# Output projection moved inside the seven-product form of the last matmuls, with its operands in float16, and the attention numerators computed two pairs ahead

## Chip, cores and metric

The kernel runs on one core of a Trainium2 chip. The metric is the device time of one execution in microseconds; the profiler's span, from the first to the last instruction of the core, is a little shorter. Engines: PE is TensorE (matmuls), DVE is VectorE, ACT is ScalarE, POOL is GpSimd, SP is SyncE, which here only issues DMAs.

## The reference

```python
def _A_ref(x, wqkv, w_phi, wo):          # S=2048, D=512, H=32 heads of Dh=16
    qkv = transpose((x @ wqkv).reshape(B, S, 3, H, Dh), 2, 0, 3, 1, 4)
    q, k, v = qkv[0], qkv[1], qkv[2]
    pq = einsum("bhsd,hdf->bhsf", q, w_phi);  pk = einsum("bhsd,hdf->bhsf", k, w_phi)
    phi_q = concat([softmax(pq), softmax(-pq)]);  phi_k = concat([softmax(pk), softmax(-pk)])
    kv  = einsum("bhsf,bhsd->bhfd", phi_k, v)
    z   = einsum("bhsf->bhf", phi_k)
    num = einsum("bhqf,bhfd->bhqd", phi_q, kv)
    den = einsum("bhqf,bhf->bhq", phi_q, z)[..., None] + 1e-6
    return reshape(num / den, (B, S, D)) @ wo

def _B_ref(x, w_gate, w_up, w_down):     # F=1792
    return ((x @ w_gate) * (x @ w_up)) @ w_down

xn = layernorm(x)
return x + _A_ref(xn, A_wqkv, A_w_phi, A_wo) + _B_ref(xn, B_w_gate, B_w_up, B_w_down)
```

All inputs are bfloat16 with batch 1. Two branches, linear attention with a softmax feature map and a gated linear unit without a nonlinearity, share the normalised input and are summed with x.

## The kernel before

**Tiles.** The 2048 tokens are 16 tiles of 128. K-blocks are 128 rows: 4 for D = 512, 14 for F = 1792. GLU units go over 4 token groups (`sg`) of 512.

**The loop** `for t in range(NT + 3)` (steps t = 0 to 18) works tile by tile: feature matmuls of k (`features("ek", ...)`), values (`v_matmul`, `v_place`), the sum over tokens `kv_acc(t - 3)` into PSUM banks 0 and 1, layernorm of later tiles, and GLU units. A unit, `up()`, is 8 matmuls of 512 columns into two of the banks 4 to 7 (in turn (4, 5) and (6, 7)), then `gate`: ScalarE copies one bank to SBUF, VectorE multiplies it with the other into `hT` (L814). From step 10 on the features of q run too (`q_next`): matmuls, two exponentials on ScalarE, a reduction on VectorE, a Ln and an Exp, two multiplications on POOL (L527, L529), and a transposing DMA into a slot of `phT` (L600). The k features end with a multiplication on POOL (L523). `w_fold` folds `w_phi` into the q and k weights.

**Scales.** h = gate x up and `w_down` are kept in float16, each multiplied by a power of two found on the chip: `squares` sums the squares of the weights (`wg`, `wu` on ScalarE at steps 3 to 9, `wd` on VectorE at steps 7 to 10, L651), `h_scale` (step 10) and `d_scale` (step 12) turn the sums into the scales `sh`, `swd` and the inverse `inv`. GLU outputs that were written before `sh` existed are converted later: those of token group 0 by `normalise` on POOL (L724, two per step from step 11; it waits for a row of reciprocal deviations that goes out to HBM and back, `r2row`), those of groups 1 and 2 by `to_half` on VectorE (L706), called after the loop and after pair 1.

**Output pairs.** The last part runs over 8 pairs p of token tiles t0 = 2p, t1 = 2p + 1. The product h @ w_down for 2 x 128 tokens and 2 x 256 columns, with F cut in two halves of 7 K-blocks, uses a form of Strassen-Winograd with 7 block products instead of 8. Sums of h blocks are made on VectorE (`h_combine`, 4 per pair, L775; three pairs ahead), sums of `w_down` blocks once (`wd_combine`, L745, `tw1` to `tw4`). `product` is 7 matmuls of 256 columns; `seed` is a ScalarE copy of one bank into another, so that partial results are used twice. The output projection o @ wo is outside of this form: `out_heads` adds 4 matmuls of 256 columns, in bfloat16, to each of the four output quarters. `finish_quarter` (L839, VectorE) scales by `inv` and adds x (or `xs`, which POOL makes at L859 from `s7` and x); `store` writes to HBM.

**Numerators.** `num_stage(t)`: 8 matmuls of 68 columns (L616) into banks 0 and 1 (tile 1: banks 2 and 3), a Ln and an Exp of the denominators on ScalarE, a division on VectorE into the tile `o` (L626), and a transposing DMA on SP (L631) that puts o transposed into the slot of `phT`. Tiles 0 and 1 run before pair 0, and tiles 2p + 2 and 2p + 3 run inside pair p, at the second and the third call of `fill()`. `fill()` of pairs 2 to 5 also runs one q feature tile each.

**Order.** TensorE runs in the order of the program. For the other engines `_order` simulates the steps with estimated costs and sorts each engine's queue, SP's included, by the modelled readiness and a priority (`sc.prio`; lower goes first). A queue, once made, is worked off in order, each instruction after the semaphores that it waits for. L224, L243 and L775 are lines of helpers (`act`, `mm`, `h_combine`), so the profile puts most ScalarE and TensorE work under one line each.

## Time and profile before

| what | value |
|---|---|
| runs | 218.68, 219.3, 220.6 us; median 219.3 |
| profiled execution | 217.15 us, span 215.3 us |
| granted TensorE clock | 1.00 |
| PE busy | 209.9 us, 97% of the span |
| DVE busy | 170.9 us, 79% |
| ACT busy | 133.7 us, 62% |
| POOL busy | 93.9 us, 44% |
| first numerators, first product of pair 0, end | about 144.4, 148.6 and 215.3 us |

Busy shares are averages over the whole span. The page also has the busy share of each engine in 40 slices of 5.4 us, the chain of work that ended last, followed back from the last instruction, groups of instructions with the mean time of one and the idle time ahead of them, and DMA issues. Further views list the instructions of a stretch in order of time and the busy time in chosen stretches. Times in a stretch count from the start of the span.

### The profile page before, as it was taken

What the parts mean: (1) busy time and instruction counts of PE and PEld (TensorE: products, weight loads), DVE (VectorE), ACT (ScalarE), POOL (GpSimd) and SP (SyncE); (2) the same over time, 40 slices, a digit from 0 to 9 for tenths busy, and PEclk for the clock granted to TensorE, in tenths of its full rate; (3) what the DMA queues carried; (4) which work ended last, traced back from release to release, by engine and by line L of the source; (5) the groups of instructions that cost most, each with busy time, mean ns of one, the idle gap of its engine ahead of it and who ended that gap; (6) DMA issues with size and microseconds to landing.
All of it is one profiled execution on the core that took longest, in us unless ns stands there. A gap on an engine that the chain in (4) does not pass through costs nothing.

```text
span 215.3 us, 3992 instructions
## 1 busy us (share of the span) xinstructions
PE 209.9 (97%) x1472; PEld 126.5 (59%) x1492; DVE 170.9 (79%) x281; ACT 133.7 (62%) x332; POOL 93.9 (44%) x112
## 2 busy tenths in 40 slices
PE   7999999999999999999999999999999999999994
PEld 2574444444444454444444444455988988989983
DVE  3838989967399999855999976869999999986332
ACT  5588869887977785876948676644333343553320
POOL 4032454530342244333999999690230523422220
PEclk9999999999999999999999999999999999999999
DMA  5999791893000000005423325255043285465731
GB/s 175 289 299 372 177 158 31 275 252 79 0 3 0 0 0 3 0 0 99 55 49 72 74 52 97 49 136 108 21 132 90 82 147 128 109 146 120 135 81 49
DMA packets 49075, 22.29 MB, mean 104 GB/s; under 512 B 38048, under 2 KB 47392, under 8 KB 49056
## 3 DMA queue, kind: packets, MB, share of 16 engines
q1 hardware_dynamic: 48112, 21.39, 43.5%
q10 hardware_dynamic: 944, 0.66, 1.0%
q8 instruction: 11, 0.18, 0.4%
q14 instruction: 8, 0.07, 0.1%
HBM read 11.03 MB, written 2.10 MB: 61 GB/s over the span
## 4 chain that ended last, share of the span: by engine, by line
PE 94%; DMA 3%; DVE 1%; issue 1%; SPq 0%; DVEq 0%
PE ps L243 89%; DMA arena<-in_A_wqkv_dram 3%; PE ps L616 2%; PE ps L559 2%; PE ps L375 1%; DVE arena L814 1%; DVE arena L775 0%; SPq L268 0%; DVE arena L839 0%; PE ps L481 0%; DVEq L1170 0%
## 5 line engine op out<-in xcount | busy, mean ns | idle before, releaser
L243 PE MATMUL ps<-arena 128*128 128x512 bf16 (+2 forms) x1156 | 200.0, 328 | 1.6 <-DMA arena<-in_A_wqkv_dram 0.5
L243 PEld LDWEIGHTS ps<-arena 128*128 128x128 bf16 (+1 forms) x1176 | 112.1, 98 | 75.7 <-ACT arena L224 1.5
L224 ACT ACTIVATE arena<-ps 128x512 bf16<-128x512 f32 (+4 forms) x119 | 59.9, 538 | 42.1 <-PE ps L243 20.0
L814 DVE TENSOR_TENSOR arena<-ps,arena 128x512 bf16<-128x512 f32 (+1 forms) x56 | 37.8, 682 | 13.0 <-PE ps L243 8.1
L523 POOL TENSOR_TENSOR arena<-arena 128x1024 bf16<-128x1024 bf16 x16 | 33.9, 2126 | 31.6 <-ACT arena L224 31.6
L513 DVE TENSOR_REDUCE arena<-arena 128x64 f32<-128x1024 bf16 x32 | 38.6, 1214 | 10.3 <-ACT arena L224 10.1
L224 ACT ACTIVATE arena<-arena 128x32 f32<-128x32 f32 (+8 forms) x119 | 40.6, 351 | 6.2 <-DVE arena L513 3.2
L224 ACT ACTIVATE arena<-ps,arena 128x512 bf16<-128x512 f32 (+1 forms) x51 | 32.5, 654 | 11.6 <-PE ps L243 10.7
L859 POOL TENSOR_TENSOR arena<-arena 128x256 f32<-128x256 f32 x16 | 11.4, 733 | 41.6 <-ACT arena L224 41.6
L839 DVE SCALAR_TENSOR_TENSOR arena<-ps,arena 128x256 bf16<-128x256 f32 x32 | 14.9, 480 | 11.6 <-PE ps L243 11.4
L724 POOL TENSOR_TENSOR arena<-arena 128x512 f16<-128x512 bf16 x14 | 19.1, 1375 | 9.3 <-DMA arena<-r2row 7.3
L775 DVE TENSOR_TENSOR arena<-arena 128x896 f16<-128x896 f16 x32 | 21.1, 674 | 0.1
L224 ACT ACTIVATE ps<-ps 128x256 f32<-128x256 f32 x24 | 8.8, 368 | 15.8 <-PE ps L243 15.5
L529 POOL TENSOR_TENSOR arena<-arena 128x512 bf16<-128x512 bf16 x16 | 17.9, 1119 | 1.3
L651 DVE SCALAR_TENSOR_TENSOR arena<-arena 128x1024 bf16<-128x1024 bf16 x7 | 13.5, 1961 | 0.2
L626 DVE TENSOR_TENSOR arena<-ps,arena 128x512 bf16<-128x512 f32 x16 | 10.9, 684 | 1.1 <-ACT arena L224 1.0
L402 DVE BATCH_NORM_STATS2 arena<-arena 128x6 f32<-128x512 bf16 x16 | 10.5, 669 | 0.0
L460 POOL TENSOR_SCALAR arena<-arena 128x1 f32<-128x1 f32 x12 | 3.2, 284 | 14.9 <-ACT arena L224 14.9
L462 DVE TENSOR_SCALAR arena<-arena 128x512 bf16<-128x512 bf16 x12 | 6.9, 604 | 1.7 <-DMA arena<-arena 1.7
L559 PEld LDWEIGHTS ps<-arena 128*128 128x128 bf16 x128 | 6.1, 97 | 3.5
L527 POOL TENSOR_TENSOR arena<-arena 128x32 f32<-128x32 f32 x16 | 4.6, 290 | 7.1 <-ACT arena L224 7.1
L616 PE MATMUL ps<-arena 128*128 128x68 bf16 x128 | 6.5, 194 | 0.0
(50 smaller groups left out, 65.5 us busy)
## 6 DMA issues: line engine op xcount, KB each, us to landing
arena<-in_A_x_dram SPq DMA_DIRECT2D x9, 256.0 KB, 3.0
out_dram<-arena SPq DMA_DIRECT2D x15, 128.0 KB, 2.0
arena<-in_B_w_down_dram SPq DMA_DIRECT2D x1, 1792.0 KB, 8.9
arena<-in_A_x_dram SPq DMA_DIRECT2D x3, 512.0 KB, 4.1
arena<-arena SPq DMA_TRANSPOSE x44, 3.0
arena<-in_B_w_gate_dram SPq DMA_DIRECT2D x1, 640.0 KB, 8.4
arena<-in_B_w_up_dram SPq DMA_DIRECT2D x1, 640.0 KB, 9.6
arena<-in_B_w_gate_dram SPq DMA_DIRECT2D x1, 512.0 KB, 5.0
```

What stands on the lines that cost most here:

```text
L224: return sc.step(ACT, lambda e: e.activation(out=out_ap, in_=in_ap, func=func, scale=scale, **kw), reads, writes, 130.0 + 0.833 * n)
L243: ins = e.matmul(out_ap, lhsT=l, rhs=r, start=start and i == 0, stop=stop and i == npair - 1, **kw)
L513: dve(lambda e: e.tensor_reduce(out=sm, in_=e_v, axis=AX.X, op=ALU.add), [(name, s, 0), (name, s, 1)], [("sums", sr)], 1024)
L523: pool(lambda e: e.tensor_tensor(out=e_w, in0=e_w, in1=r_w, op=ALU.mult), [(name, s, 0), (name, s, 1), ("rs", n)], [(name, s, 0), (name, s ...
L529: pool(lambda e: e.tensor_tensor(out=e_v[:, :, 1, :], in0=e_v[:, :, 1, :], in1=rat[:, :, None].to_broadcast([128, H, 16]), op=ALU.mult), [ ...
L626: dve(lambda e: e.tensor_tensor(out=o_tile(t).rearrange("p (b h f) -> p b h f", b=2, f=16), in0=nd[:, :, :, 0:16], in1=w_v[:, r].unsqueeze ...
L651: dve(lambda e: e.scalar_tensor_tensor(out=junk, in0=i_ap, scalar=1.0, in1=i_ap, op0=ALU.mult, op1=ALU.mult, accum_out=ssq[:, col:col + 1] ...
L724: pool(lambda e, ft=ft: e.tensor_tensor(out=hH_v[:, ft, 0:512], in0=hT_v[:, ft, 0:512], in1=r2w, op=ALU.mult), [("hT", ft, 0), "r2w", ("x" ...
L775: dve(lambda e, k=k, i0=i0, i1=i1, op=op: e.tensor_tensor(out=s_block(p, k), in0=i0, in1=i1, op=op), ks + more, [s_key(p, k)] + over.get(k ...
L814: dve(lambda e: e.tensor_tensor(out=h_v[:, ft, sg * 512:(sg + 1) * 512], in0=bank(bu), in1=g, op=ALU.mult), [("ps", bu), ("g", s)] + ([("j ...
L839: dve(lambda e: e.scalar_tensor_tensor(out=stg, in0=bank(b, 0, 256), scalar=inv, in1=resid, op0=ALU.mult, op1=ALU.add), [("ps", b), rkey, ...
L859: pool(lambda e, h=h: e.tensor_tensor(out=xs[h], in0=s7, in1=xr_tile(t1)[:, h * 256:(h + 1) * 256], op=ALU.add), ["s7", ("xr", t1 % 4)], [ ...
```

## The change

- The projection goes into the seven products: each product has 9 K-blocks, 7 of h with `w_down` and 2 of o with `wo`. `out_heads` goes away. For this o and wo become float16, with a common scale: `squares` of `wv` and `wo` on ScalarE (steps 9 and 10), a longer `d_scale`, which finds `so`, `swo`, `swd` and `inv` under caps, and two conversions of `wo` on VectorE. `kv_finish` scales the key-value sums by `so`.
- `combine_weights` makes the sums of both weights (`tw`, `two`) on VectorE, at steps 16 and 17 and after the loop; the third is made in place.
- `o_combine(p)` makes four sums of o blocks on POOL for each pair, in the free parts of the `phT` slots.
- Numerators of tiles 0 to 3 run before pair 0, with one GLU unit after each of the first three; pair p >= 1 runs tiles 2p + 4 and 2p + 5, at its first and second `fill()`; pair 0 runs 4 and 5.
- `to_half` goes from VectorE to ScalarE, one conversion per step from step 11.
- Squares, `w_fold(0, ...)` and `normalise` run one step earlier; `q_next` is spread over steps 9 to 18, and the last four q tiles run in pairs 0 to 3; step 14 has one GLU unit less.
- The bank numbers of the products change; two of the four finishing instructions of a pair become one over two banks, and the two `xs` instructions become one.

The core of the diff:

```diff
@@ num_stage's o is now float16; scales
     def o_tile(t):
-        return sb("o", (t % 3) * 512, 512)
+        return sbh("o", (t % 3) * 512, 512)
...
     def d_scale():
-        norms(14, 7, 1)
-        power_of_two(swd, scl[:, 18:19], [("rn", 14)], "swd", 4096.0)
-        dve(lambda e: e.tensor_tensor(out=scl[:, 22:23], in0=sh, in1=swd, op=ALU.mult), ["sh", "swd"], ["both"], 1)
-        dve(lambda e: e.reciprocal(out=scl[:, 23:24], in_=scl[:, 22:23]), ["both"], ["rboth"], 1)
-        power_of_two(inv, scl[:, 23:24], ["rboth"], "inv", 1.0009765625)
-        sc.prio = 2
+        norms(14, (2, 2, 7), 24)
...
+        for i in range(2):
+            sl = slice(2 * i, 2 * i + 2)
+            dve(lambda e, sl=sl: e.tensor_scalar(out=woh_v[:, sl, :], in0=wo_v[:, sl, :], scalar1=swo, scalar2=None,
+                                                 op0=ALU.mult), ["wo", "scales"], [("woh", i)], 1024, 0.35)
...
     def to_half(sg):
         fts = [ft for ft in range(NF) if (ft, sg) in raw]
-        sc.prio = 2
         for lo in range(0, len(fts), 2):
...
-            dve(lambda e, sl=sl: e.tensor_scalar(out=hH_v[:, sl, sg * 512:(sg + 1) * 512],
...
+            act(hH_v[:, sl, sg * 512:(sg + 1) * 512], hT_v[:, sl, sg * 512:(sg + 1) * 512],
+                ks + ["sh", ("hT", *latest[0])], ks, func=ACTF.Identity, scale=sh)
+            yield
...
+    def o_combine(p):
+        t0, t1 = 2 * p, 2 * p + 1
+        a11, a12, a21, a22 = (o_block(t, i) for t in (t0, t1) for i in range(2))
+        ks = [("phT", t0), ("phT", t1)]
+        for k, i0, i1, op, more in ((1, a21, a22, ALU.add, []),
+                                    (3, a11, a21, ALU.subtract, [1]),
+                                    (2, so_block(p, 1), a11, ALU.subtract, [1]),
+                                    (4, a12, so_block(p, 2), ALU.subtract, [2])):
+            pool(lambda e, k=k, i0=i0, i1=i1, op=op: e.tensor_tensor(out=so_block(p, k), in0=i0, in1=i1, op=op),
+                 ks + [("so", p, m) for m in more], [("so", p, k)], 256)
...
-    BA, BE, BB, BC, BD = 3, 7, 4, 5, 6
+    BA, BE, BD, BB, BC = 3, 5, 6, 7, 4
+
+    def product(b, a, w, start=False):
+        h, o, keys, okey = a
+        wh, wo_, wkeys = w
+        mm(bank(b, 0, 256), [(h[:, f, :], wh[:, f, :]) for f in range(NK)],
+           keys + wkeys + ([] if start else [("ps", b)]), b, start=start, stop=False, skip=True)
+        mm(bank(b, 0, 256), [(o[:, f, :], wo_[:, f, :]) for f in range(2)], [okey, ("ps", b)], b, start=False, skip=True)
...
+        product(BA, raw_a(t0, 0), raw_w(0, 0), True)
         seed(BB, BA)
         fill()
+        product(BE, sum_a(3), sum_w(3), True)
+        act(s7, ...); pool(xs = s7 + x, ...)
+        product(BB, sum_a(2), sum_w(2))
         seed(BD, BB)
+        fill()
+        product(BA, raw_a(t0, 1), raw_w(1, 0))
+        finish(t0, 0, 256, ...)
+        product(BB, sum_a(1), sum_w(1))
+        seed(BC, BB)
         fill()
+        product(BD, raw_a(t1, 1), sum_w(4))
+        finish(t1, 0, 512, ...)
+        product(BC, sum_a(4), raw_w(1, 1))
+        finish(t0, 256, 256, ...)
...
@@ after the loop
     h_combine(0)
-    wd_combine(4)
+    combine_weights(4)
...
-    num_stage(0)
-    up(len(ups) - 2)
-    num_stage(1)
-    up(2)
-    h_combine(1)
-    to_half(1)
-    h_combine(2)
-    h_combine(3)
+    for t in range(4):
+        num_stage(t)
+        up((1, 1, 1, len(ups))[t])
+        half_step(1)
+    half_step(99)
+    o_combine(0)
+    for p in range(1, 4):
+        h_combine(p)
     for p in range(NT // 2):
-        plan = [[], [2 * p + 2], [2 * p + 3]]
+        plan = [[2 * p + 4], [2 * p + 5], []] if p else [[], [4], [5]]
...
-            if 1 < p < 6 and len(plan) == 2:
+            if p < 4 and not plan:
                 q_next(2)
         out_pair(p, fill)
-        if p == 1:
-            to_half(2)
+        if p + 1 < NT // 2:
+            o_combine(p + 1)
```

## The prediction

> **What bounds the kernel now.** I read the page first: busy shares, slices, the chain that ended last.
>
> ```profile
> PE 209.9 (97%) x1472; PEld 126.5 (59%) x1492; DVE 170.9 (79%) x281; ACT 133.7 (62%) x332; POOL 93.9 (44%) x112
> PE   7999999999999999999999999999999999999994
> DVE  3838989967399999855999976869999999986332
> POOL 4032454530342244333999999690230523422220
> PEclk9999999999999999999999999999999999999999
> PE 94%; DMA 3%; DVE 1%; issue 1%; SPq 0%; DVEq 0%
> ```
>
> TensorE is busy from the second slice to the last, at a granted clock of 1.00 throughout, and it is 94% of the chain. VectorE is nearly full in the last third (slices 28 to 35, the output pairs) without being the chain. So a saving must take columns off TensorE, and an added wait costs only if it reaches TensorE. The list of waits, asked for TensorE alone from 20 us on, is empty. The windows cut at each pair's first numerator say the same (columns: stretch, its length, then busy time and instructions of PE, PEld, DVE, ACT and POOL, the granted clock, DMA share, GB/s):
>
> ```profile
> 152.15:159.76 7.61, 7.61 (x84) 6.86 (x81) 7.36 (x16) 2.43 (x8) 1.48 (x2) 1.00 0.27 69
> 168.23:176.70 8.47, 8.42 (x87) 7.26 (x85) 7.95 (x14) 3.68 (x12) 3.04 (x5) 1.00 0.59 95
> 193.64:201.25 7.61, 7.61 (x84) 6.88 (x82) 3.27 (x6) 2.63 (x10) 2.84 (x5) 1.00 0.70 120
> ```
>
> A pair takes 7.61 us, or 8.47 with a q feature tile in it. The last row has VectorE at 3.27 us instead of 7.36 and is no shorter: in the pairs VectorE sets nothing. The chain in order of time gives TensorE's price list:
>
> ```profile
> 152.31 0.26 PE ps L616 x8
> 152.57 2.40 PE ps L243 x22
> 154.97 0.26 PE ps L616 x8
> 155.23 4.69 PE ps L243 x43
> ```
>
> 22 matmuls of 256 columns in 2.40 us and 43 in 4.69 are both 0.1091 us each; a numerator tile (8 matmuls) is 0.26. Check: 65 x 0.1091 + 2 x 0.26 = 7.61, the window's length. A GLU unit (8 matmuls of 512 columns) is 1.73 us in the same view.
>
> **What is removed.** Before, a pair is 7 products of 7 matmuls and 4 groups of 4 for the output projection: 49 + 16 = 65. After, it is 7 x (7 + 2) = 63. Eight pairs: 16 matmuls x 0.1091 = **1.75 us** off the engine that is the chain. Halves in float16 bring no more: products in f16 and projection groups in bf16 both stand at 273 ns in the table of forms, and the stretch of 43 that mixes them ran at the same 0.1091 as the others. Splitting a product into two waiting steps costs nothing that shows, since the same stretch has such borders already.
>
> One page would make this term smaller. The Trainium skill, TensorE: Matmul & The Clock Gate, section Back-to-back issue gap, gives a sustained spacing of 81 ns at 128 columns and 131 at 512; halfway in columns that is an estimated 98 ns and 1.57 us. This trace has 216 ns at 512 (1.73 / 8), so the measurement decides.
>
> **What is added to POOL.** The sums of o: 4 subtractions per pair of 128x256 f16, each reading two SBUF operands and mostly waiting for the one before. No such row exists; the nearest are these.
>
> ```profile
> L859 POOL TENSOR_TENSOR arena<-arena 128x256 f32<-128x256 f32 x16 | 11.4, 733 | 41.6 <-ACT arena L224 41.6
> 158.55 2.12 POOL L859 TENSOR_TENSOR arena<-arena 128x256 f32<-128x256 f32 x2 [6.13 <-ACT arena L224]
> 175.70 1.30 POOL L859 TENSOR_TENSOR arena<-arena 128x256 f32<-128x256 f32 x2 [4.20 <-ACT arena L224]
> L724 POOL TENSOR_TENSOR arena<-arena 128x512 f16<-128x512 bf16 x14 | 19.1, 1375 | 9.3 <-DMA arena<-r2row 7.3
> ```
>
> Low end 0.65 us (1.30 for two), high end 1.06 (2.12 for two, while VectorE was working on f16 tiles); the longest single L859 was 1.49. I take 0.75, near the L859 mean. POOL per pair: 4 x 0.75 + 1.5 (residual and s7, same elements in one instruction) + 1.4 (the q tile's 0.27 + 1.1) = 5.9 us in a pair of 63 x 0.1091 + 0.52 + 0.86 = 8.25. It fits; with 1.06 throughout it is 4.2 + 2.1 + 1.8 = 8.1 and just fits. The sums for pair p+1 read tiles whose numerators run in pair p-1, so they have about a pair of lead, except for pair 0.
>
> A page speaks against this edit. The Trainium skill, SBUF — State Buffer, section Who interferes with whom: a VectorE instruction with two SBUF inputs and a GpSimd one that reads SBUF exclude each other for the whole instruction. The rows agree in kind (L775 on VectorE runs from 0.61 to 1.37 us, L859 from 0.67 to 1.49). By the rule a POOL op could wait out an L775 (0.62) each time, an estimated 1.3 us an op; the whole change would then come out slower.
>
> **Pair 0.** Now four numerator tiles and three GLU units precede it: 4 x 0.26 + 3 x 1.73 = 6.23 us from the first numerator to its first product. The path of one tile, in the rows of ScalarE, VectorE and SP around 168 us:
>
> ```profile
> 168.23 0.42 PE L616 MATMUL ps<-arena 128*128 128x68 bf16 x8
> 169.36 0.68 DVE L626 TENSOR_TENSOR arena<-ps,arena 128x512 bf16<-128x512 f32 x1
> 170.07 1.19 SPq L631 DMA_TRANSPOSE arena<-arena  x1
> ```
>
> Start of the numerators to the DMA's issue: 1.84 us; landing after 2.4 more (the line's minimum and median; maximum 4.6). Tile 1 starts at 0.26 + 1.73 = 1.99, so its o lies in SBUF at 6.23. Its sums S1 and S3 end at 6.23 + 2 x 0.75 = 7.73. The third-product group that reads S3 comes after 9 + 7 matmuls, at 6.23 + 1.75 = 7.98. This wait is new, and all of TensorE queues behind it; next in line, S2 is wanted 0.98 later and takes 0.75, so nothing piles up. Low end 0, high end 2.6 us (landing 4.6, sums 1.06: 1.99 + 1.84 + 4.6 + 2.12 - 7.98). I take 0.2, near the low end, for semaphore time is not in the sum.
>
> **Numerators two pairs ahead.** Within a pair they now stand 0.26 + 18 x 0.1091 = 2.22 us apart instead of 2.66, on the same banks 0 and 1. The second must wait until L626 has read the first: start to end of L626 was 1.81 (168.23 to 170.04), 1.81, 1.93, 1.99 and once 2.28 (152.15 to 154.43). Late by 0 to 0.1 per pair, six pairs: 0 to 0.6; I take 0.05. Each also brings its Ln and Exp (0.20, 0.23), its L626 and a 1.19 us transpose on SP. SP per pair: 2 x 1.19 + 1.24 + 2 x 0.55 + 0.43 = 5.2 us of 8.25, unchanged. The q tiles of pairs 2 to 5 go to 0 to 3 whole; their 0.86 us of TensorE merely moves.
>
> **The loop before the pairs.** ScalarE gets four squares of 1.04 + 0.19 = 4.9 us and the nine half conversions of hT (eight of 1.04, one of 0.6: 8.9 us), which VectorE loses (4.1 us in the pairs). ScalarE was busy 28.85 of 40 us from 80 to 120 and 13.75 of 20 after: about 70%, then 85 to 90%. A conversion can hold a gate back by 1.04. A gate needs 0.69 (ScalarE) + 0.68 (VectorE) + some 0.25, and its banks return two units later: at least one unit of 1.73, and in the new order 0.86 of features or values more, so about 1 us is free. Low end 0, high end 0.2 at each of eight steps, 1.6; I take 0.1. On VectorE two wo conversions (0.82 each), four small differences (0.4 each, scaled from 0.674 at 896) and some eight scale instructions of 0.16 add 4.5 us; before, 16.0 of 20 us were busy from 120 to 140, so it stays hidden, and the differences are wanted only in pair 0. The longer chain of scales starts near 100 us and is read at 141. The weight fold one step earlier finds its transposes landed (issued at 27.5, 6.7 to land, wanted past 47). The normalisation one step earlier still waits for r2row, landed at 100.5; behind it on POOL stand the k products, read three steps of 8 us later. A GLU unit less at step 14 is one of the three before pair 0.
>
> **Sum.** -1.75 + 0.2 + 0.05 + 0.1 = -1.4 us. Against the profiled execution (217.15 us, span 215.3): 215.75, span 213.9. The median of the runs, 219.3, lies 1% above that execution; the same -1.4 gives **217.9 us**, 0.6% less. The tail (last product, 0.48 of VectorE, about 2 us of store) stays.
>
> **Rivals.** (1) *More than the sum:* TensorE's small idle times between 28 and 201 us add to 1.1 us, and VectorE, 95% busy in the pairs, is relieved. All gone and no new wait: -2.85, 216.4. Against it: the last window above, where free VectorE brought nothing. (2) *The saving goes into pair 0:* with a landing near 4.6 us and sums near 1.06, 2.6 us are lost there: -1.75 + 2.6 + 0.15, 220.3; with half of it 219.0. For it: POOL also has the last q tiles then. Against: the median landing is at the minimum. (3) *Slower: POOL paces the pairs.* From a mean of 1.09 us per sum on, POOL needs more than the 8.25 us of a pair with a q tile. At 1.2, between the contended 1.06 and the longest 1.49, it is 4.8 + 2.4 + 1.8 = 9.0, 0.75 late in each of four pairs, and 7.2 against 7.39 in the others: +3.0 - 1.4 = +1.6, 220.9; at 1.3 it is 9.6 and 7.8, +6.6 - 1.4 = +5.2, 224.5. For it: both engines' long rows when they overlap. Against: six of the eight L859 pairs are near 1.3 us. (4) *Little is won:* conversions hold gates up at each step, 1.6 us lost: 219.3.
>
> **How the numbers follow.** Forecast 0.47, (1) 0.21, (2) 0.12, (3) 0.13, (4) 0.07. One per cent is about what a measurement can tell from no change. Faster: all of (1), and 0.06 of the forecast where no new wait appears: 0.27. Slower: (3), and 0.05 of (2) and (4) at their ends: 0.18. The rest, 0.55, is within 1%. The forecast's own range is 217.3 to 219.2; the wider one goes to (1) below, 216.2, and to (2) and the mild half of (3) above, 220.9.
>
> **What would show it.** Right: 536 matmuls of 256 columns instead of 552, a pair without q of 7.4 us and with q of 8.25, POOL sums of 0.65 to 0.85, and TensorE's wait list naming POOL at pair 0 at most, under 0.5 us. Wrong: TensorE waiting on POOL in later pairs (3), on L626 at L616 (spacing), or on gates between 93 and 145 us (4); or a loop longer than before by the time the first numerator starts, less the moved GLU unit.

## The result and the profile after

The changed kernel takes **227.1 us** (median; 226.6 to 229.2), the kernel before 219.05 in the same comparison: a ratio of 1.037, 95% interval 1.029 to 1.046. Forecast were 217.9 us and a range up to 220.9. The profiled execution took 226.6 us with a span of 224.8, so 9.5 us more than the 215.3 of before. The page of the changed kernel, with the rows that answer to those shown of before:

```profile
PE 211.0 (94%) x1476; PEld 124.5 (55%) x1476; DVE 178.8 (80%) x276; ACT 144.6 (64%) x349; POOL 116.4 (52%) x138
PE   7999999999999999999967899997689999999995
DVE  3848999953899997658999999998899987985223
POOL 4032654343034425509965999815839747566620
PEclk9999999999999999999999999999999999999999
PE 60%; DVE 27%; issue 5%; ACT 4%; DMA 3%; POOL 1%; DVEq 0%; POOLq 0%
```

TensorE has holes in two places, the 21st to 23rd slice of 5.62 us (112 to 129 us: the loop) and the 28th to 30th (152 to 169 us: the start of the pairs). VectorE reads 9 in and ahead of the first, and 8, 8 and 9 in the second, and the chain that was 94% TensorE is now 27% VectorE. The granted clock of this execution is 1.00 throughout; of the four timed ones only the slowest, 229.2 us, has a mean below it, 0.985. The list of waits for TensorE from 20 us on, empty before, now reads:

```profile
PE ps L616 <- DVE arena L626: 4.1, 5, 2.4
PE ps L243 <- DVE arena L860: 2.3, 2, 1.5
PE ps L243 <- ACT arena L224: 2.0, 2, 1.7
PE ps L243 <- POOL arena L822: 1.4, 1, 1.4
```

(total us, number of waits, longest.) L860 is `gate` (before: L814), L822 `o_combine`, L800 `h_combine` (before: L775), L889 `finish` (before: `finish_quarter`, L839).

**Where the 9.5 us lie.** The first numerators of the kernel before, then rows of the changed kernel (the bracket holds the idle time ahead of a row and what ended it):

```profile
144.43 0.67 PE L616 MATMUL ps<-arena 128*128 128x68 bf16 x16
```
```profile
147.38 0.42 PE L616 MATMUL ps<-arena 128*128 128x68 bf16 x8
157.71 1.38 PE L243 MATMUL ps<-arena 128*128 128x256 f16 x11 [1.41 <-POOL arena L822]
163.66 0.43 PE L616 MATMUL ps<-arena 128*128 128x68 bf16 x8 [2.36 <-DVE arena L626]
```

The first numerator starts at 147.38 us, before at 144.43, although one GLU unit of 1.73 fewer stands ahead of it: the loop is 2.95 + 1.73 = 4.7 us longer. From there to the end it is 77.4 us (224.8 - 147.4) against 70.9 (215.3 - 144.4). With one unit more (+1.73) and 16 matmuls fewer (-1.75) it should have been 70.9 again: the pairs are 6.5 us longer. 4.7 + 6.5 - 1.75 = 9.5. TensorE's own rows show idle times of 4.3 us in the loop (0.25, 1.47, 0.84, 1.72) and 5.7 behind it, the largest 1.41 and 2.36 in pair 0. They add to 10.0 of 11.2. A row's end is modelled, and in an undisturbed stretch the next row starts some 0.17 us before it, so each of these eleven holes is up to that much longer than its number.

### The profile page after: what moved, and what is told of

The parts are those of the page before. It is cut to its first block, busy times and chain, and to the rows that moved or that the text cites. A ratio compares the mean times of both kernels' runs of the same rounds, so it can differ in the third digit from the quotient of the medians.

```text
span 224.8 us, 4025 instructions
## 1 busy us (share of the span) xinstructions
PE 211.0 (94%) x1476; PEld 124.5 (55%) x1476; DVE 178.8 (80%) x276; ACT 144.6 (64%) x349; POOL 116.4 (52%) x138
## 4 chain that ended last, share of the span: by engine, by line
PE 60%; DVE 27%; issue 5%; ACT 4%; DMA 3%; POOL 1%; DVEq 0%; POOLq 0%
PE ps L243 56%; DVE arena L513 6%; DVE arena L800 5%; DVE arena L860 4%; ACT arena L224 4%; DVE arena L771 3%; DVE arena L718 3%; DVE arena L889 2%; DVE arena L626 2%; DMA arena<-arena 1%; DMA arena<-in_A_x_dram 1%; PE ps L559 1%; PE ps L616 1%; POOL arena L822 1%; DVE arena L672 1%
## 5 line engine op out<-in xcount | busy, mean ns | idle before, releaser
L243 PEld LDWEIGHTS ps<-arena 128*128 128x128 bf16 (+1 forms) x1160 | 110.3, 98 | 80.8 <-ACT arena L224 3.5
L224 ACT ACTIVATE arena<-arena 128x32 f32<-128x32 f32 (+8 forms) x132 | 53.9, 423 | 17.6 <-DVE arena L513 10.4
L523 POOL TENSOR_TENSOR arena<-arena 128x1024 bf16<-128x1024 bf16 x16 | 34.0, 2129 | 28.6 <-ACT arena L224 28.5
L860 DVE TENSOR_TENSOR arena<-ps,arena 128x512 bf16<-128x512 f32 (+1 forms) x56 | 37.8, 682 | 12.4 <-ACT arena L224 6.4
L513 DVE TENSOR_REDUCE arena<-arena 128x64 f32<-128x1024 bf16 x32 | 38.6, 1209 | 4.0 <-ACT arena L224 3.8
L822 POOL TENSOR_TENSOR arena<-arena 128x256 f16<-128x256 f16 x32 | 23.7, 749 | 19.8 <-DMA arena<-arena 19.1
L800 DVE TENSOR_TENSOR arena<-arena 128x896 f16<-128x896 f16 x32 | 26.4, 846 | 2.6 <-POOL arena L822 1.9
L889 DVE SCALAR_TENSOR_TENSOR arena<-ps,arena 128x256 bf16<-128x256 f32 (+1 forms) x24 | 13.5, 566 | 11.9 <-PE ps L243 11.9
L743 POOL TENSOR_TENSOR arena<-arena 128x512 f16<-128x512 bf16 x14 | 17.4, 1262 | 10.4 <-DMA arena<-r2row 7.9
L529 POOL TENSOR_TENSOR arena<-arena 128x512 bf16<-128x512 bf16 x16 | 18.4, 1148 | 0.9
L626 DVE TENSOR_TENSOR arena<-ps,arena 128x512 f16<-128x512 f32 x16 | 10.9, 683 | 4.8 <-ACT arena L224 4.8
L918 POOL TENSOR_TENSOR arena<-arena 128x512 f32<-128x512 f32 x8 | 10.8, 1354 | 5.7 <-ACT arena L224 5.7
L527 POOL TENSOR_TENSOR arena<-arena 128x32 f32<-128x32 f32 x16 | 5.7, 354 | 13.9 <-ACT arena L224 11.6
L616 PE MATMUL ps<-arena 128*128 128x68 bf16 x128 | 6.7, 194 | 4.3 <-DVE arena L626 4.1
L616 PEld LDWEIGHTS ps<-arena 128*128 128x128 bf16 x128 | 5.7, 97 | 7.0 <-DVE arena L626 5.0
```

What stands on the lines that cost most here:

```text
L224: return sc.step(ACT, lambda e: e.activation(out=out_ap, in_=in_ap, func=func, scale=scale, **kw), reads, writes, 130.0 + 0.833 * n)
L243: ins = e.matmul(out_ap, lhsT=l, rhs=r, start=start and i == 0, stop=stop and i == npair - 1, **kw)
L513: dve(lambda e: e.tensor_reduce(out=sm, in_=e_v, axis=AX.X, op=ALU.add), [(name, s, 0), (name, s, 1)], [("sums", sr)], 1024)
L523: pool(lambda e: e.tensor_tensor(out=e_w, in0=e_w, in1=r_w, op=ALU.mult), [(name, s, 0), (name, s, 1), ("rs", n)], [(name, s, 0), (name, s ...
L529: pool(lambda e: e.tensor_tensor(out=e_v[:, :, 1, :], in0=e_v[:, :, 1, :], in1=rat[:, :, None].to_broadcast([128, H, 16]), op=ALU.mult), [ ...
L616: ins = e.matmul(bank(b0 + c // 4, (c % 4) * CW, CW), lhsT=ph[:, c, :], rhs=kvz_v[:, c, :], start=True, stop=True)
```

## Experiments

Two theories for the loop. *Order*: the nine conversions of weights, now at the same priority as the gates, stand ahead of more urgent work in VectorE's queue. *Load*: VectorE has too much to do there, whatever its order. Two for the pairs: the numerators' new *spacing*, or *the sums of o* on POOL, which would make VectorE's work on two SBUF operands longer. Edits are against the changed kernel unless the kernel before is named; all ratios are to the kernel before.

**The saving by itself (on the kernel before).** Two matmuls are left out of each pair: the last K-block of o @ wo for the odd token tile.

```diff
-    mm(bank(b, 0, 256), [(oT_tile(t)[:, q, :], wo_v[:, q, ...]) for q in range(NQ)], ...
+    mm(bank(b, 0, 256), [(oT_tile(t)[:, q, :], wo_v[:, q, ...]) for q in range(NQ - t % 2)], ...
```

> The kernel before with two matmuls per pair left out (the last K-block of o @ wo for the odd tile, both halves), so that part of the projection is missing from the output: 63 instead of 65 matmuls of 256 columns per pair, the same number that the changed kernel has, and nothing else. If the columns of TensorE are what sets the pairs of the kernel before, 16 x 0.109 = 1.75 us less, 0.8%. If VectorE at 95% in the pairs would have been next at once, less than 0.7 us.

Measured: 215.3 us, ratio 0.988 (0.983 to 0.993), and still no wait of TensorE from 20 us on. The profiled spans, 213.5 against 215.3, differ by 1.8 us, the predicted 1.75. The medians differ by 2.9, but the kernel before scatters there from 216.6 to 219.6 us, and the interval, 1.5 to 3.8 us, holds the prediction. The term that the change is made for is real; all else has to be explained beside it.

**Order of the conversions.** First alone in the kernel before, whose seven conversions go to priority 1 instead of 2:

```diff
@@ kernel before, d_scale
-        sc.prio = 2
```

> The kernel before with one edit: its seven conversions of w_down (L696) lose priority 2 and stand at 1 as in the changed kernel. Theory A (the priority alone suffices to stop TensorE): 2 to 4 us slower than before, TensorE idle between 105 and 125 us. Theory B (it takes the longer scale chain and the added work too): less than 1 us slower.

Measured: 218.7 us, ratio 1.0025 (0.998 to 1.007), with TensorE idle 0.87 and 0.25 us in the loop; its profiled span of 216.8 us lies among those of the kernel before, 214.8 to 217.7. The priority alone makes no difference in time that the runs show. Then the opposite in the changed kernel, around the nine conversions:

```diff
@@ d_scale
+        sc.prio = 2
         for i in range(2):
...
+        sc.prio = 1
```

> The changed kernel with one edit: the conversions of wo and w_down to float16 (L714, L718) get priority 2 again, behind the reductions and gates in VectorE's modelled queue. Theory A (the block of nine conversions, 111.7 to 120.2 us in the changed kernel, holds up the reductions L513, behind them the gates on ScalarE, and so TensorE, which stood idle 4.3 us between 113 and 125 us): those 4.3 us go, device time 3.5 to 4.5 us under the changed kernel's. Theory B (VectorE and POOL shut each other out, and VectorE simply has too much to do from 100 to 165 us, in any order): the backlog only moves, at most 1 us less. Theory C (the closer numerators wait for L626): nothing in the pairs changes, at most 4.5 us less.

Measured: 229.6 us, ratio 1.052 (1.044 to 1.061): slower still, with a hole of 3.92 us at 113.8, after which the clock fell (last section), and others of 1.09 and 0.40 later in the loop. The simple form of the order theory falls.

**Order of the loop's steps.** Squares, folds, `normalise`, `q_next` and the unit of step 14 are put back where they were; of the edit, the squares, the unit and one call of `q_next`:

```diff
-        if 2 <= t < 9:   squares("wg", t - 2, last); squares("wu", t - 2, last)
+        if 3 <= t < 10:  squares("wg", t - 3, last); squares("wu", t - 3, last)
...
-            if t != 14:
-                up()
-            if t in (13, 15):
-                q_next()
+            up()
+            q_next()
...
```

> The changed kernel with the order of work in the loop put back to that of before: GLU units, q features (two per step from 12 to 16), squares, weight folds and half conversions of group 0 on the steps that they had; the scales, the conversions on ScalarE and the pairs stay as changed. Theory O (the new order put reductions and gates against the conversions): the idle time between 105 and 130 us goes, 3 to 5 us less than the changed kernel. Theory L (long small instructions and added conversions on VectorE): they are still there, less than 1.5 us either way.

Measured: 228.9 us, ratio 1.048 (1.042 to 1.055); the loop's idle times are 0.96, 1.58, 1.41, 0.47, 0.63 and 0.25 us, 5.3 together instead of 4.3. The moved steps are not the cause.

**The chain of scales.** VectorE's rows in order of time in the changed kernel show what runs ahead of the late gates:

```profile
102.89 1.03 DVE L672 TENSOR_SCALAR arena<-arena 128x3 f32<-128x3 f32 x1
...
106.99 1.30 DVE L706 SCALAR_TENSOR_TENSOR arena<-arena 128x1 f32<-128x1 f32 x1
...
109.45 1.08 DVE L673 TENSOR_SCALAR arena<-arena 128x3 int32<-128x3 int32 x1
...
113.30 3.33 DVE L718 TENSOR_SCALAR arena<-arena 128x1024 f16<-128x1024 bf16 x4
116.56 0.68 DVE L860 TENSOR_TENSOR arena<-ps,arena 128x512 f16<-128x512 f32 x1
117.16 3.07 DVE L718 TENSOR_SCALAR arena<-arena 128x1024 f16<-128x1024 bf16 x3
120.15 1.21 DVE L513 TENSOR_REDUCE arena<-arena 128x64 f32<-128x1024 bf16 x1
```

These instructions on one to three numbers per partition take about a microsecond. POOL is busy with tensors in SBUF all the while (rows of L743, L523 and L529 from 101.6 on; two of them):

```profile
106.34 1.94 POOL L523 TENSOR_TENSOR arena<-arena 128x1024 bf16<-128x1024 bf16 x1
108.22 3.41 POOL L743 TENSOR_TENSOR arena<-arena 128x512 f16<-128x512 bf16 x3
```

Each long one ends where an instruction of POOL ends: L706 at 108.29 us with L523 at 108.28, L673 at 110.53 with the second of the three L743 (1.14 each, so 110.5). Its length is what was left of POOL's instruction. The same kinds that began near such an end took 0.14 to 0.19 us (L702 on 128x3 at 102.70, L673 at 103.96, L705 on two 128x1 tensors at 105.19). From 111.69 to 120.15 VectorE does its nine conversions and one gate. Only then comes the reduction L513 of a feature tile, and ScalarE and TensorE, rows of the same stretch, wait for that and for the gates:

```profile
121.39 0.50 ACT L224 ACTIVATE arena<-arena 128x32 f32<-128x32 f32 x2 [5.49 <-DVE arena L513]
117.29 1.90 PE L243 MATMUL ps<-arena 128*128 128x512 bf16 x8 [1.47 <-DVE arena L860]
124.77 6.22 PE L243 MATMUL ps<-arena 128*128 128x512 bf16 x28 [1.72 <-ACT arena L224]
```

The edit: the same scales found one column at a time, each instruction but a reciprocal with one column and a single tensor operand, and without the row of gains that POOL wrote.

```diff
-        power_of_two(scl[:, 38:41], scl[:, 38:41], ["p3"], "caps", 1.0)
...
-        power_of_two(scl[:, 42:45], scl[:, 42:45], ["rup"], "inv", 1.0009765625)
+        for i, gain in enumerate((256.0, 4096.0, 4096.0)):
+            power_of_two(col(38 + i), col(32 + i), [("rn", 14)], ("caps", i), gain)
+        one(col(41), so, col(39), ALU.mult, ...); one(rise, col(40), sh, ALU.mult, ...); one(rise, rise, col(41), ALU.min, ...)
+        for i in range(3):
+            power_of_two(col(42 + i), col(42 + i), ["rup"], ("inv", i), 1.0009765625)
+        one(swd, col(43), rise, ALU.mult, ...); one(swo, col(44), rise, ALU.mult, ...)
```

> The changed kernel with its chain of scales written as instructions of one column and one tensor operand each (18 small instructions instead of 10 that take two or three columns, or two tensors). In the changed kernel L672, L673, L706 and L710 took 0.61 to 1.30 us each between 102.9 and 111.7 us while POOL was busy; the one-column kind took 0.15 before. Theory L (what waits for POOL is the form: several columns or two tensor operands): all 18 near 0.15 us, the conversions start some 3 us earlier, TensorE's 4.3 us of idle time between 113 and 125 us fall under 1.5: 3 to 4 us less than the changed kernel. Rival (any VectorE instruction there waits for POOL, or the added conversions are the load): the small ones stay at 0.6 us or more, or the idle time only moves; less than 1 us.

Measured: 18 small instructions instead of 9, and each takes 0.14 to 0.21 us beside the same work on POOL:

```profile
108.27 0.21 DVE L672 TENSOR_SCALAR arena<-arena 128x1 f32<-128x1 f32 x2
108.45 0.21 DVE L673 TENSOR_SCALAR arena<-arena 128x1 int32<-128x1 int32 x2
```

So it is the form beside POOL's work, not the number, that cost a microsecond each. The Trainium skill orders these rows: by VectorE: DVE Perf Modes, section What auto-detection actually checks, one source and a destination in SBUF run on both ports if their outermost dimensions of more than one element are equal or both even, and by SBUF — State Buffer, section Who interferes with whom, such an instruction and a GpSimd one, or one with two SBUF tensors and a GpSimd one that reads SBUF, shut each other out for their whole length. The runs agree for these forms: TENSOR_SCALAR on 128x3 up to 1.08 us and two tensors 1.30, 128x1 with one tensor 0.15. Not every instruction on three columns waits: the reciprocal on 128x3 (L711 of this run) took 0.18 us in the midst of POOL's L523. The conversions start 2.4 us earlier (109.26) and the first numerator 2.3 us earlier (145.11), but the time is 226.5 us, ratio 1.038 (1.028 to 1.047). The conversions themselves became longer beside POOL (four of them 5.35 us, against 0.47 for one with POOL idle), and the waits from the first numerator on come to 6.1 us instead of 5.7. A dip of the clock (last section) takes another 1.5: the 31 matmuls behind the longest wait needed 5.43 us instead of 3.97. A gain at one place was not handed on to the end.

**The load of the conversions.** All nine go to ScalarE, at priority 2 (`wo` shown, `wd` likewise):

```diff
+        sc.prio = 2
-            dve(... tensor_scalar(out=woh_v[:, sl, :], in0=wo_v[:, sl, :], scalar1=swo ...), ..., 1024, 0.35)
+            act(woh_v[:, sl, :], wo_v[:, sl, :], ["wo", "scales"], [("woh", i)], func=ACTF.Identity, scale=swo)
...
+        sc.prio = 1
```

> The changed kernel with the nine conversions of wo and w_down on ScalarE (1.04 us each, priority 2) instead of VectorE. In the changed kernel they take VectorE from 111.7 to 120.2 us but for one gate, with ScalarE idle 5.5 us behind the reduction that comes after them. Theory D (the added VectorE work of this stretch, these conversions above all, is what the gates and TensorE wait for; with the conversions merely put last, e1, it only moved): the idle time of TensorE between 110 and 130 us falls from 4.3 us to under 1.5, the first numerators start 3 to 4 us earlier than at 147.4, and the time is 3 to 5 us less than the changed kernel's. Rival (ScalarE was the tight one in the loop, as the prediction's fourth rival had it): gates come later still, no gain or up to 3 us more.

Measured: the loop's idle times fall from 4.3 us to 0.44, and the first numerator starts at 143.01, 4.4 us earlier. That is the loss in the loop, all but 0.3 us: **VectorE's load** causes it. The edit takes away all nine conversions, the seven old ones too, so it doesn't say how much each added piece weighs; the chain of scales alone gave 2.3 us above. The time is 227.4 us all the same, ratio 1.038 (1.032 to 1.044). The queue of VectorE, and TensorE, tell why:

```profile
154.01 1.06 DVE L800 TENSOR_TENSOR arena<-arena 128x896 f16<-128x896 f16 x1 [1.84 <-DMA arena<-arena]
154.99 4.68 DVE L771 TENSOR_TENSOR arena<-arena 128x1792 f16<-128x1792 f16 x4
```
```profile
143.01 0.42 PE L616 MATMUL ps<-arena 128*128 128x68 bf16 x8
158.25 3.88 PE L243 MATMUL ps<-arena 128*128 128x256 f16 x18 [5.94 <-DVE arena L771]
```

At low priority the conversions are spread to the end of the loop and beyond (on ScalarE instructions of their form, which is that of the half conversions too, start as late as 149.96 us). The four sums of `w_down` blocks (L771), done by 141.6 us in the changed kernel, came when pair 0 already wanted them: 5.94 us lost in one place. The 18 matmuls behind it took 3.88 us instead of 2.13, for the clock stood at 0.50 from 155 to 160 us. So the loop gives 4.4 us, the waits from the first numerator on cost 3.7 more than in the changed kernel, the clock costs 1.75, and the span is 1.0 longer.

**Spacing of the numerators.** Second and third call of `fill()` in every pair, as before:

```diff
-        plan = [[2 * p + 4], [2 * p + 5], []] if p else [[], [4], [5]]
+        plan = [[], [2 * p + 4], [2 * p + 5]]
```

> The changed kernel with one edit: inside every pair the two numerator tiles run at the second and third fill (as before the change), still two pairs ahead; they then stand 0.26 + 18 x 0.109 = 2.2 us apart again but after the products BB and BB2, and the first of them comes 1.96 us later in the pair. Theory C (the waits of L616 for L626, 2.36 + 0.51 + 0.49 + 0.45 = 3.8 us in the changed kernel, come from where the numerators stand): 1.5 to 3.8 us less than the changed kernel. Theories A and B (L626 is late because VectorE's queue is): the waits stay or move, -0.5 to +1 us.

Measured: 225.8 us, ratio 1.037 (1.028 to 1.046), span -1.0. The waits of 0.51, 0.49 and 0.45 us on L626 in pairs 1, 2 and 4 become 0.20 in one pair and none; the 2.36 of pair 0 stays (2.32). By the spans and the idle times the spacing costs 1.0 to 1.3 us, and is the smaller part; the ratios to the kernel before, 1.037 for both, don't tell the two apart.

**Without the sums of o.** `o_combine` is not called; the products wait for the transposed o instead of its sums.

```diff
-    o_combine(0)
...
-        if p + 1 < NT // 2:
-            o_combine(p + 1)
```

> The changed kernel with the four POOL sums of o per pair left out: the products read o as it stands, so the projection's part of the output isn't that of the reference, and its time is that of a kernel without these 32 POOL instructions (23.7 us of POOL). Theory B (they lock VectorE out: L800 went from 0.674 to 0.846 us mean, and from 0.61 to as much as 1 us in the pairs): L800 returns to 0.70 or less, and 3 to 6 us of the 6.5 us lost in the pairs come back. Theories A and C: only the wait of TensorE for L822 at pair 0 (1.4 us) and little more goes, 1 to 2 us less; the loop, 4.7 us longer than before, stays as it is under all three.

Measured: 222.6 us, ratio 1.019 (1.009 to 1.030). From the first numerator to the end it is 72.1 us instead of 77.4: the sums cost **5.3 us of the 6.5** lost in the pairs. 1.41 us of it is TensorE's own wait for the first sums; the rest comes by way of VectorE: the wait of 2.36 us for L626 becomes 0.84, and those of pairs 1, 2 and 4 go. The groups by form, first of the changed kernel, then of this one:

```profile
L800 DVE TENSOR_TENSOR arena<-arena 128x896 f16<-128x896 f16 x32 | 26.4, 846 | 2.6 <-POOL arena L822 1.9 <-PE ps L243 0.5
L822 POOL TENSOR_TENSOR arena<-arena 128x256 f16<-128x256 f16 x32 | 23.7, 749 | 19.8 <-DMA arena<-arena 19.1
```
```profile
L800 DVE TENSOR_TENSOR arena<-arena 128x896 f16<-128x896 f16 x32 | 19.9, 643 | 2.4 <-DMA arena<-arena 1.8 <-PE ps L243 0.5
```

POOL's 0.749 us per sum is what was predicted. Not priced was what it does to VectorE: a sum of h blocks takes 0.846 us instead of 0.643, and in pair 0, where both engines have a row of them, more:

```profile
158.33 4.68 DVE L800 TENSOR_TENSOR arena<-arena 128x896 f16<-128x896 f16 x5 [1.94 <-POOL arena L822]
162.93 0.68 DVE L626 TENSOR_TENSOR arena<-ps,arena 128x512 f16<-128x512 f32 x1
```

That is 0.94 us each, beside the end of POOL's first set of four sums (156.23 to 159.49), its L918 and the start of the second set (3.48 us from 161.69). Without the sums three of them took 1.70 us, 0.57 each. L626, for which TensorE waits 2.36 us, stands behind them in VectorE's queue. No run put L626 ahead of them, so how much of the 2.36 us the order of that queue would give back stays open.

**The idle 1.94 us ahead of those five.** The fourth sum of h blocks of pair 0 has its place in a slot that q tile 10 still holds; its transposing DMA could be what VectorE waited for. Another slot:

```diff
-            for k, name, lo in ((1, "vs", 0), (2, "vs", NK * 128), (4, "eq", 1024))}
+            for k, name, lo in ((1, "vs", 0), (2, "vs", NK * 128), (4, "ph2", 7 * 1024))}
```

> The changed kernel with one edit: the fourth h sum of pair 0 goes into a free tile of x instead of slot 1 of eq, so it no longer waits for the transposing DMA of q tile 10 (issued at 154.97 us, landing some 3 us later; VectorE stood idle 1.94 us until 158.33). Theory Q (this wait, at the head of VectorE's queue, makes L626 late and TensorE stand 2.36 us at 163.66): those 2.36 us fall to 0.6 or less, 1.7 to 2.4 us less than the changed kernel. Rival (VectorE's slow L800, 0.94 us each there beside POOL's sums, do it): 0.5 us less or none.

Measured: the idle time is gone, so the profile's releaser (POOL L822) was not the true one; the run without the sums of o names a DMA for the same wait. But the sums now run beside POOL's first set, six in 6.14 us, 1.02 each. TensorE still waits 1.98 us for L626, and the time is 228.6 us, ratio 1.047 (1.039 to 1.054), with two dips of the clock in it (last section). The 2.36 us fall by 0.4, as the rival had it: the DMA is not the cause, and the longer sums take the time back.

**Sums of o on VectorE.**

```diff
-            pool(lambda e, ...: e.tensor_tensor(out=so_block(p, k), in0=i0, in1=i1, op=op), ...)
+            dve(lambda e, ...: e.tensor_tensor(out=so_block(p, k), in0=i0, in1=i1, op=op), ..., 256, 0.55)
```

> The changed kernel with the four sums of o per pair on VectorE instead of POOL (same operands, 128x256 f16). Theory B (POOL's sums and VectorE's f16 instructions shut each other out): the 32 sums cost 0.25 to 0.3 us each on VectorE, 1.1 us per pair, L800 returns to 0.65 to 0.7 us, and 2 to 4 us of the 6.5 us lost in the pairs come back. Rival (VectorE is simply full in the pairs): 1.1 us more per pair on it makes numerators and finishing later still, 0 to 4 us more than the changed kernel.

Measured: 0.422 us a sum, L800 back to 0.702, the 2.36 gone, but 1.72 us for the third sum of pair 0 and 0.16 to 0.33 in four later pairs. The profiled execution, at a clock of 0.999, has a span of 222.6 us, 2.2 less than the changed kernel; the other four, at 0.991 or 0.992, have 224.4 to 224.7, so the median is 226.3 us, ratio 1.036 (1.029 to 1.044), with 224.3 as the fastest. At a like clock the low end of the expected 2 to 4 us is there, by one execution. VectorE pays 13.1 us for the sums and gets 5.0 back.

**Together.** First all that had helped at one place: one-column scales, conversions on ScalarE at priority 2, sums of o on VectorE, the old spacing. The edits are those shown above under these four names.

> The changed kernel with four edits together: scales in one-column instructions, the nine conversions on ScalarE, the sums of o on VectorE, and the numerators of each pair at its second and third fill. If VectorE's load in the loop (theory D), the exclusion with POOL (theories B and L) and the place of the numerators (theory C) are the causes of the 11 us, and the saving of 16 matmuls is real, TensorE's idle time after 20 us falls from 10 us to 3 or less: 216 to 218 us, near the kernel before, at best 1% under it. If each only hands its delay to the next wait, 221 us or more.

Measured: 231.3 us, ratio 1.056 (1.052 to 1.061). The loop has no idle time left (first numerator at 142.72), and the pairs have 4.95 us for the late weight sums, then 1.47, 1.18 and 2.04: VectorE never catches up. The clock falls to 0.50 behind the first and to 0.73 behind the last of these waits, some 3.5 us more. The next version gives each piece of work a time: conversions on ScalarE, three at each of the steps 13 to 15, half conversions after the loop and after pair 1, where they were before (but on ScalarE), the other slot for the fourth sum, sums of o on VectorE; spacing as in the changed kernel.

```diff
+        if 13 <= t < 16:
+            conv_step(3)
...
-        if t >= 11:
-            half_step(1)
...
+    halves.append(to_half(1))
```

> The changed kernel with these edits: scales in one-column instructions; the nine conversions of wo and w_down on ScalarE, three at each of the steps 13 to 15 (so that the sums of the weights at step 16 find them done); the half conversions of hT out of the loop and back to where they were (before pair 0 and after pair 1), on ScalarE at priority 2; the fourth h sum of pair 0 in a free tile of x; the sums of o on VectorE. Theory D plus B (VectorE's load and its exclusion with POOL are the whole loss): first numerators near 143 us as in the run with conversions on ScalarE, no wait of 5 us for the weight sums at pair 0, total idle of TensorE after 20 us under 3 us, 216 to 219 us. If the delay is handed on once more, 221 us or more, and the wait list names where.

Measured: **222.6 us**, ratio 1.019 (1.013 to 1.026), the best version of the change as a whole. Its nine idle times are all 0.26 to 1.08 us, 5.9 together, and the clock is 0.999 or 1.000 in all four executions. With 0.17 us hidden in each they come to 7.4; less the 1.75 saved that is 5.7, and the span is 5.4 us longer than that of the kernel before: the saving is there, and only the waits are lost. The same with POOL's sums and the old spacing:

```diff
-            dve(lambda e, ...: e.tensor_tensor(out=so_block(p, k), in0=i0, in1=i1, op=op), ..., 256, 0.55)
+            pool(lambda e, ...: e.tensor_tensor(out=so_block(p, k), in0=i0, in1=i1, op=op), ...)
...
-        plan = [[2 * p + 4], [2 * p + 5], []] if p else [[], [4], [5]]
+        plan = [[], [2 * p + 4], [2 * p + 5]]
```

> The same as the spread version, but with the sums of o on POOL as in the changed kernel, and the numerators of each pair at its second and third fill. Theory B: POOL's sums lengthen L800 again to 0.8 us or more and cost 2 to 4 us in the pairs against the version with the sums on VectorE. Rival (in the pairs VectorE was late only because the loop handed its backlog on): with the loop mended both versions lie within 1 us of each other.

Measured: 223.8 us, ratio 1.023 (1.016 to 1.030); the sums of h blocks take 0.966 us beside POOL's sums and 0.659 without. The 2 to 4 us expected of the place of the sums aren't there: the intervals overlap, and the two spans at a clock of 1.00, 220.4 and 221.6, lie around the 220.7 to 220.9 of the version before. 10.0 us less for sums of h stand against 15.9 us for sums of o on VectorE. The spacing differs too, so the two are not separated here. Last, a finer spread, against the best version: two conversions per step from 12 to 16, half conversions two per step from 16 to 18, one after each early numerator, and none in the pairs.

```diff
-        if 13 <= t < 16:
-            conv_step(3)
+        if 12 <= t < 17:
+            conv_step(2)
...
+        if t >= 16:
+            half_step(2)
```

> The spread version with the sums on VectorE, and the work on ScalarE spread further: conversions of w_down and wo two per step from step 12 to 16, half conversions of hT two per step from step 16 to 18 and one after each of the first numerators, none in the pairs. Theory: what is left in the spread version (0.64 + 0.76 us behind blocks of conversions in the loop, 0.92 us for a seed behind half conversions in pair 0) goes, 1.5 to 2.5 us less than its 222.6, 220 to 221 us; the waits on L626 (2.5 us in five places) and for the sums of pair 0 (1.1 us) stay, for they come from the numerators' places and VectorE's queue. Rival (any order only hands the wait on): no change or slower.

Measured: 225.0 us, ratio 1.033 (1.027 to 1.039), with idle times of 0.49, 1.02, 1.66 and 2.13 us ahead of the pairs. The wait only moves: the 2.13 us end with ScalarE, the 1.66 with a gate that stands in VectorE's queue behind three sums of `wo` blocks (4.05 us from 136.42). No version here beats the kernel before; whether some order of the queues keeps the whole 1.75 us stays open.

## Why the prediction was wrong

- **Removed: right.** -1.75 predicted, -1.8 measured alone. After, the last stretch has 162 matmuls in 17.7 us, 0.109 each, and the table of forms 504 + 32 = 536 matmuls of 256 columns. (In the estimate that the prediction sets aside, 256 columns stand a third of the way from 128 to 512, which is what its 98 ns is, not halfway.) The one pair whose numerators waited for nothing shows the predicted length (column two):

```profile
185.58:193.83 8.25, 8.25 (x85) 7.06 (x83) 6.67 (x11) 3.69 (x12) 5.32 (x7) 1.00 0.52 126
193.83:201.83 8.00, 7.55 (x81) 6.61 (x79) 6.70 (x11) 2.70 (x10) 5.78 (x7) 1.00 0.74 123
```

  8.25 us with a q tile, as forecast. The pair after it, without one, should have taken 7.4 and took 8.00, with 0.45 idle and the 0.17 that a row's end hides.
- **VectorE's added work "add 4.5 us; before, 16.0 of 20 us were busy from 120 to 140, so it stays hidden": the step that failed in the loop.** +0.1 us forecast for the loop, +4.7 measured. Both halves were wrong. The size: nine scale instructions took 5.6 us instead of 1.3 for some eight, the four `wo` differences 3.6 (0.915 each) instead of 1.6; the two `wo` conversions were right (1.7). The seven old conversions went from 5.4 to 6.4. All told VectorE gained 7.9 us of busy time though it gave 4.1 away: +12. The place: the cover was read from 120 to 140 us, a mean over 20 us, but of this work only the `wo` differences lie there; the scales and conversions fall into one block at 103 to 120 us, where the gates and a reduction are due. And the price of the loop was looked for on ScalarE, which stood idle for 5.49 us there, waiting for VectorE. The trace of before had a warning: its L682, one VectorE instruction on two 128x1 tensors, took 1.88 us where its neighbours took 0.15, and ended at 86.2 us with POOL's L523.
- **POOL's sums: right as a price, wrong as a cost, the step that failed in the pairs** and the larger loss: +0.25 us forecast for pair 0 and the spacing, +6.5 measured from the first numerator on. 0.75 us each forecast, 0.749 measured; POOL did not pace the pairs (rival 3). But the price was counted on POOL alone. The rule of exclusion was quoted and applied to POOL's side; VectorE's side, +0.17 us on each of 32 sums of h (0.846 against 0.674 before), was not in the sum. The sums cost 5.3 us by their removal. The step "in the pairs VectorE sets nothing" rested on a pair in which it had slack, and at pair 0 it has none.
- **Pair 0: 0.2 forecast, 1.41 measured** for the first sums, inside the given 0 to 2.6, but the reason was another: the second numerator's L626 ran at 152.17, behind a reduction and a gate, instead of at 150.8 (1.13 after its numerators, as in the kernel before at 168.23), and its transpose landed 3.2 us after its issue instead of 2.4. The next wait there, 2.36 us, was not forecast at all; L626 stood behind five sums.
- **Spacing: 0.05 forecast, 1.0 to 1.3 measured.** Sign and place were right (L626 at L616, 0.45 to 0.51 in three pairs). The start-to-end of L626 had been read from a VectorE without POOL's sums beside it.
- **The rivals.** None had VectorE as the engine that becomes the bound, so the range ended 6.2 us short. (Its low end stands as 216.2 where rival 1 comes to 216.4.) The listed sign of error, "a loop longer than before by the time the first numerator starts, less the moved GLU unit", is what was seen.

## What to carry to other kernels

Work added to an engine that is "80% busy" isn't hidden by the mean: put it into the windows where it will stand, with what is queued behind it, and let the consumer of that queue set the price. When two engines shut each other out, an operation moved to one is paid on both, so cost the other engine's instructions again at the longer duration, tiny ones too. And undo parts in pairs: several edits here mended their own place entirely (4.4 us in the loop) and gave nothing at the end, since the next late block and the clock took it.

## What was not expected of the hardware

After waits of TensorE the granted clock fell in some executions, at times after short ones. In the run without the sums of o, idle times of 0.85 and 1.71 us within 4 us (and 1.48 some 4 us earlier) were followed by this (window, length, PE and the other engines, clock ahead of the last two columns):

```profile
125.00:130.00 5.00, 4.53 (x15) 1.81 (x16) 4.78 (x6) 4.39 (x12) 4.87 (x5) 0.67 0.48 92
```

28 matmuls of 512 columns took 7.59 us there instead of 6.22. The run with the other slot for the fourth sum fell to 0.67 at the same place and to 0.66 at 165 us after its 1.98, the one with one-column scales to 0.78 and 0.88 after 2.44. Long waits were followed by a dip each time: 3.92 us with conversions last (0.83 over 10 us), 4.95 in the first version together and 5.94 with conversions on ScalarE (0.50 over 5 us). The profiles of the changed kernel, of the old spacing and of the sums on VectorE have the same idle times in the loop at a clock of 1.00, so the short ones do not bring it each time. The Trainium skill, TensorE: Matmul & The Clock Gate, section Part 1: The HAM clock gate, gives at least one idle window of about 3.4 us as the condition for the half clock; here single waits of 1.71 to 2.44 us were sometimes enough.

A dip costs 1.4 to 1.9 us beyond the wait itself, by the rows behind it (7.59 us for 6.22, 5.43 for 3.97, 4.02 for 2.13). Executions of one and the same kernel show it too: without the sums of o the spans are 220.0 and 220.1 us at a mean clock of 1.00, 221.6 and 222.1 at 0.992. So part of the difference between versions is the clock and not their order of work. The best version keeps a clock of 0.999 or 1.000 in all its executions; no execution of those with conversions last, one-column scales, the other slot or conversions on ScalarE reaches 0.993.
